# Moving two exact subtractions to TensorE and shortening a hand-built exponential, in an attention and mixture-of-depths kernel

## The chip, the cores and the metric

The kernel runs on one core of a Trainium2 chip. The metric is the device time of one execution in microseconds, the median of several runs. A core has TensorE (PE, matrix products into PSUM), VectorE (DVE) and ScalarE (ACT) for elementwise work, GpSimd (POOL), and SyncE (SP), which here only issues transfers. Each engine takes its own instructions in their order; semaphores hold an instruction until what it reads has been written.

## What is computed

There are B = 8 batches, H = 8 heads, S = 576 positions, 64 elements a head and 32 memory slots. The heads' outputs, side by side, are the rows x of the second part.

```python
a = phi - np.max(phi, axis=2, keepdims=True)
a = np.exp(a)
a = a / (np.sum(a, axis=2, keepdims=True) + 1e-09)
k_m = np.einsum('bhsm,bhsd->bhmd', a, k)
v_m = np.einsum('bhsm,bhsd->bhmd', a, v)
scores = scale * np.matmul(q, k_m.transpose(0, 1, 3, 2))
scores = scores - np.max(scores, axis=-1, keepdims=True)
attn = np.exp(scores)
attn = attn / (np.sum(attn, axis=-1, keepdims=True) + 1e-09)
return np.matmul(attn, v_m).astype(np.float32)
...
scores = np.einsum('bsd,d->bs', x, w_gate)
top_idx = np.argpartition(-scores[b], capacity)[:capacity]
...
ye = np.maximum(xe @ w1, 0.0) @ w2
out[b, top_idx] = x[b, top_idx] + g[:, None] * ye
```

The first softmax runs over the 576 positions, the second over the 32 slots; capacity is 128 of 576 rows. Which 128 rows are chosen depends on the last bits of x. That is why the kernel takes the first softmax and the sums `v_m` with more care than plain float32 products give: it builds its own exponential, and splits both factors of `v_m` into a high part (the low 12 bits masked off) and a low part (the rest).

## The kernel before

**Groups.** The first softmax works on 16 groups, one per batch and half of the heads: a tile of 128 rows (4 heads x 32 slots) and 576 columns. `softmax(i, ch)` (L182 to L279) is a generator; each `yield` ends one of its eleven steps. It takes the maximum and subtracts it (L192, L194), reduces the argument by a multiple q of ln 2 (L197 to L200), and forms exp(r) - 1 as a quotient of two polynomials `num` and `den`. `fma` (L216 to L225) is one step of a polynomial in split arithmetic: six DVE instructions on 128x576, with the high part of the running value in an int16 tile (`vh` or `dh`) that ACT rounds. It is used once for `den` (L229) and three times for `num` (L236). The reciprocal of `den` comes from two squares on ACT, `sq` (L242) and `s2` (L249), with L247 between them, and is applied in L257 and L258. L259 to L276 add the leading part `y0` (an exponential rounded to int16), multiply by the power of two, and divide by the sum. L276 writes the finished group, `e`.

**keys.** `keys` (L308 to L339) goes on from there: PE transposes `e` in six pieces (L316), ACT copies them out of PSUM (L318), DVE masks the high part (L322) and subtracts it to get the low one (L324), GpSimd issues eight stores to `aparts` (L327), and PE forms k_m with float32 products (L333).

**split_v.** `split_v` (L281 to L304) does the same for v, 16 tiles of 128x1152: load, mask (L293), subtract (L295), two stores to `vparts` (L298). Its two tile names have two buffers each.

**values.** `values(st)` (L343 to L383) then sums v_m for two batches at a time, four sets in all: 2304 small products a set (L371), which read both split factors back from memory in 32 pieces (L350, L357).

**The later work.** `attention(b)` makes the second softmax, the outputs and the ranking of the rows, and `ffn` the two weight products (L636, L646) on the chosen rows.

**The order.** Nothing is scheduled by the hardware or a planner: the loop at L747 interleaves the generators turn by turn, and the order of that loop is the order on every engine. In a turn, `softmaxes` takes one step. Two softmax chains run at once for the first eight groups (a new one may start six rounds after the last); the other eight groups run one after another in chain 0. `split_v` takes a step on every odd turn (L755), the value sums take 7, 10 or 12 steps of eight products (L712), and, once chain 1 has ended and all of v is split (L759), `attentions` takes a step, and `ffns` two. The tiles of PSUM named `bank` come from a pool of four buffers, in turn. Because each engine keeps this order, an instruction that waits holds up all that was written behind it, of whatever generator.

Of the kernel before, what the change touches and what calls it, by code (L numbers as in the profile page):

```python
# [8 lines left out]
F32 = mybir.dt.float32  # L9
# [17 lines left out]

LOG2E = 1.44269504088896341
# [5 lines left out]
Y0_SCALE = 12 * 0.6931471805599453  # L34
# [3 lines left out]
def kernel(  # L38
# [76 lines left out]
    make_identity(nc, ident)  # L115

# [52 lines left out]
    UP, GRID = 2.0 ** 23, 2.0 ** -11  # L169
    biases = {}  # L170
    for x in (EXP_P[3] * UP, EXP_P[4] * UP, EXP_P[3] * UP * GRID, EXP_Q[1] * UP,
              EXP_Q[1] * UP * GRID, 127 * UP, -1.5, Y0_SCALE):
        biases[x] = constant(x)
# [8 lines left out]
    def softmax(i, ch):  # L182
# [27 lines left out]
        tt(out=num, in0=num, in1=r, op=ALU.mult)  # L210
        vh = t("vh", I16)
        act(vh, num, GRID, EXP_P[3] * UP * GRID)
        act(num, num, 1.0, EXP_P[3] * UP)
        stt(out=rl, in0=rh, scalar=-GRID, in1=r, op0=ALU.mult, op1=ALU.add)

        def fma(val, h, c):  # L216


            lo, big, low = t("lo"), t("big"), t("low")
            stt(out=lo, in0=val, scalar=GRID, in1=h, op0=ALU.mult, op1=ALU.subtract)  # L220
            tt(out=lo, in0=lo, in1=rh, op=ALU.mult)  # L221
            tt(out=big, in0=h, in1=rh, op=ALU.mult)
            tt(out=low, in0=val, in1=rl, op=ALU.mult)
            tt(out=low, in0=low, in1=lo, op=ALU.add)  # L224
            stt(out=val, in0=big, scalar=c * UP, in1=low, op0=ALU.add, op1=ALU.add)  # L225
# [5 lines left out]
        act(dh, den, GRID / 2)  # L231
        y0 = t("y0", I16)
        act(y0, r, 1.0, Y0_SCALE, AF.Exp)
        for c in (EXP_P[2], EXP_P[1], EXP_P[0]):
            yield
            fma(num, vh, c)  # L236
            if c != EXP_P[0]:
                vh = t("vh", I16)
                act(vh, num, GRID)
            if c == EXP_P[2]:  # L240
                sq = t("rl2")
                act(sq, den, 1.0 / UP, -1.5, AF.Square)  # L242


        dl, p = t("lo"), t("big")
        stt(out=dl, in0=den, scalar=GRID / 2, in1=dh, op0=ALU.mult, op1=ALU.subtract)
        stt(out=p, in0=sq, scalar=0.75, in1=den, op0=ALU.add, op1=ALU.mult)  # L247
        s2 = t("low")
        act(s2, p, 1.0 / UP, -1.5, AF.Square)  # L249
# [7 lines left out]
        stt(out=num, in0=s2, scalar=0.75, in1=num, op0=ALU.add, op1=ALU.mult)  # L257
        stt(out=num, in0=sq, scalar=0.75, in1=num, op0=ALU.add, op1=ALU.mult)  # L258
        stt(out=num, in0=num, scalar=GRID, in1=y0, op0=ALU.mult, op1=ALU.add)  # L259
        sm = ex.tile([P, 4], F32, name="sm")  # L260
        e = t("e")
        stt(out=e, in0=num, scalar=GRID / 2, in1=two_q.bitcast(F32),
# [15 lines left out]
        yield  # L278
        yield from keys(i, ch)  # L279

    def split_v():  # L281
# [6 lines left out]
        coming = load(*groups[0])  # L288
        for i, (b, g) in enumerate(groups):
            vb = coming  # L290
            yield
            hi = vio.tile([P, 4 * S * Dh // P], F32, name="vhi")
            nc.vector.tensor_single_scalar(hi.bitcast(I32), vb.bitcast(I32), -4096,  # L293
                                           op=ALU.bitwise_and)
            nc.vector.tensor_sub(vb, vb, hi)  # L295
            yield
            for vp, src in enumerate((vb, hi)):
                nc.gpsimd.dma_start(  # L298
                    out=vparts[b, g, :, vp].rearrange("w r s d -> w (r s d)")
                                           .rearrange("w (p x) -> p w x", p=P),  # L300
                    in_=src.unsqueeze(1).to_broadcast([P, 2, 4 * S * Dh // P]))
            if i + 1 < len(groups):
                coming = load(*groups[i + 1])
            yield  # L304

    v_m = {}

    def keys(i, ch):  # L308
# [15 lines left out]
        nc.vector.tensor_sub(lo, aS, hi)  # L324
# [422 lines left out]
    while True:  # L747
# [7 lines left out]
        if len(working) == 2 and turn % 2:  # L755
# [71 lines left out]
```

## Time and profile before

| | |
|---|---|
| median of three runs | 1050.5 us (1049.24 to 1057.09) |
| span of the profiled run | 1051.3 us |
| end of L276 for group 1, 5, 9, 16 | 58.3, 216.5, 377.1, 790.5 us |
| v splits (L295) | from 21.3 to 347 us |
| first and last value product | 185 to 937 us, in four sets |
| moved by transfers | 166.11 MB, 158 GB/s over the span |

The end of L276 is the mark to go by: it is the moment at which a group of the first softmax is finished, and everything later (transposes, stores, value sums, attention) waits for it. Up to 377 us two chains share DVE and a group comes about every 40 us; from there to 790 us one chain runs beside attention and the feed-forward part, and a group comes about every 59 us. What follows 790 us has no work of the first softmax in it.

In the lines of the profile, a group names its line, engine, operation, tiles (written <- read) and shape; then come the total and the mean time of one, and the idle time of the engine before it with what ended that. A duration of idle time is a cost only where the engine sets the pace.

### The profile page before, as it was taken

The numbers are of one execution on the slowest core, as the hardware profiler recorded it, in microseconds if no ns is written. First come the engines' busy times: TensorE is split into PE (matmuls) and PEld (weight loads), VectorE is DVE, ScalarE is ACT, GpSimd is POOL, SyncE is SP. The second block draws the span as 40 slices with busy tenths as digits, with TensorE's granted clock in tenths as the row PEclk, the third lists the DMA queues.
The fourth block names the chain that finished last, engine by engine and source line by source line (L and its number), as shares of the span: only waits on it lengthen the run. The fifth ranks groups of instructions, "written<-read, shape, count | busy, mean of one in ns | idle before, by whom it ended". The sixth has DMA issues, their size and how long they took to land. (4 is left out here: it accounts for less than half of the span.)

```text
span 1051.3 us, 25384 instructions
## 1 busy us (share of the span) xinstructions
PE 598.7 (57%) x10738; PEld 439.8 (42%) x10738; DVE 784.4 (75%) x1342; ACT 293.6 (28%) x578; POOL 224.3 (21%) x335
## 2 busy tenths in 40 slices
PE   0021022255554355675567397875738969889795
PEld 0021022154443354554434374664415657544542
DVE  7899999899899968698786968698993336324940
ACT  2233233233233232323224342141432101213230
POOL 7030221220230230404113021402503011011110
PEclk9999999995665656877678699566866986989688
DMA  9364544677887825554613256463404466522320
GB/s 291 126 232 153 188 157 169 192 230 277 264 274 253 313 46 155 152 179 145 214 51 106 72 141 206 127 194 115 114 0 116 153 218 189 163 66 66 120 70 23
DMA packets 60714, 166.11 MB, mean 158 GB/s; under 512 B 10801, under 2 KB 21041, under 8 KB 60593
## 3 DMA queue, kind: packets, MB, share of 16 engines
q1 hardware_dynamic: 39088, 94.14, 29.5%
q0 software_dynamic: 21504, 70.27, 19.7%
q8 instruction: 87, 1.43, 0.6%
q14 instruction: 35, 0.28, 0.1%
HBM read 96.21 MB, written 68.16 MB: 156 GB/s over the span
## 5 line engine op out<-in xcount | busy, mean ns | idle before, releaser
L371 PE MATMUL acc<-a_rows,v_rows 32*64 32x128 f32 x9216 | 217.8, 257 | 106.7 <-DMA a_rows<-aparts 97.6
L371 PEld LDWEIGHTS acc<-a_rows,v_rows 32*64 32x64 f32 x9216 | 197.7, 167 | 150.2 <-issue 113.9
L316 PE MATMUL bank<-ident,e 128*96 128x128 f32 x96 | 22.5, 403 | 214.8 <-DVE e L276 204.6
L316 PEld LDWEIGHTS bank<-ident,e 128*96 128x96 f32 x96 | 16.0, 185 | 219.7 <-issue 183.4
L333 PE MATMUL bank<-lo,kb 96*128 96x64 f32 x384 | 67.0, 353 | 7.6 <-ACT lo L318 6.8
L333 PEld LDWEIGHTS bank<-lo,kb 96*128 96x128 f32 x384 | 65.5, 267 | 12.1 <-ACT lo L318 8.6
L327 POOL DMA_DIRECT2D aparts<-low x64 | 47.2, 746 | 104.5 <-DVE low L324 100.8
L646 PE MATMUL bank<-w_sb,hT 128*128 128x512 f32 x128 | 67.2, 661 | 0.0
L636 PE MATMUL bank<-w_sb,xeT 128*128 128x512 f32 x128 | 65.5, 647 | 2.9 <-ACT xeT L627 2.9
L530 PE MATMUL bank<-vbd,eT 128*128 128x256 f32 x160 | 60.0, 510 | 0.0
L221 DVE TENSOR_TENSOR lo<-lo,rh 128x576 f32<-128x576 f32 x64 | 56.7, 885 | 2.2
L176 ACT ACTIVATE vh<-num 128x576 int16<-128x576 f32 x32 | 21.8, 683 | 127.3 <-DVE num L225 116.7
L534 DVE TENSOR_TENSOR xj<-bank,rd 128x512 f32<-128x512 f32 x40 | 27.5, 688 | 36.8 <-PE bank L530 34.9
L537 POOL TENSOR_TENSOR xj<-xj,mean 128x1024 f32<-128x1024 f32 (+1 forms) x12 | 26.1, 2174 | 128.5 <-DVE xj L534 89.8
L583 DVE SCALAR_TENSOR_TENSOR cmp<-row,tg,wide 128x576 bf16<-128x576 f32 x40 | 32.5, 811 | 25.9 <-ACT row L569 25.1
L298 POOL DMA_DIRECT2D vparts<-vb x16 | 11.6, 726 | 186.2 <-DVE vb L295 161.9
L224 DVE TENSOR_TENSOR low<-low,lo 128x576 f32<-128x576 f32 x64 | 48.5, 758 | 2.2
L327 POOL DMA_DIRECT2D aparts<-big x64 | 46.7, 738 | 0.0
L220 DVE SCALAR_TENSOR_TENSOR lo<-num,vh 128x576 f32<-128x576 f32 x48 | 36.0, 751 | 13.2 <-ACT vh L176 13.2
L530 PEld LDWEIGHTS bank<-vbd,eT 128*128 128x128 f32 x160 | 35.0, 243 | 23.8 <-issue 19.6
L602 PE MATMUL bank<-tg,pick 128*128 128x2 f32 (+1 forms) x80 | 16.9, 329 | 47.4 <-DVE pick L597 20.2
L176 ACT ACTIVATE low<-big,c 128x576 f32<-128x576 f32 x16 | 12.4, 775 | 96.4 <-DVE big L247 96.4
(150 smaller groups left out, 1244.2 us busy)
## 6 DMA issues: line engine op xcount, KB each, us to landing
v_rows<-vparts SPq DMA_DIRECT2D x128, 288.0 KB
vparts<-vb POOLq DMA_DIRECT2D x16, 1152.0 KB, 5.2
vparts<-vhi POOLq DMA_DIRECT2D x16, 1152.0 KB, 8.9
a_rows<-aparts SPq DMA_DIRECT2D x512, 36.0 KB
vb<-in_v SPq DMA_DIRECT2D x16, 576.0 KB
kb<-in_k SPq DMA_DIRECT2D x16, 576.0 KB
qb<-in_qT SPq DMA_DIRECT2D x16, 576.0 KB
out<-xj POOLq DMA_DIRECT2D x16, 512.0 KB, 3.8
```

The lines of the kernel that those rows point to most:

```text
L176: nc.scalar.activation(dst, src, func, bias=biases[c] if c else 0.0, scale=s)
L220: stt(out=lo, in0=val, scalar=GRID, in1=h, op0=ALU.mult, op1=ALU.subtract)
L221: tt(out=lo, in0=lo, in1=rh, op=ALU.mult)
L224: tt(out=low, in0=low, in1=lo, op=ALU.add)
L316: nc.tensor.transpose(out=tp[:, c], in_=a[:, (c0 + c) * PT:(c0 + c + 1) * PT], identity=ident)
L327: nc.gpsimd.dma_start(out=aparts[h, b, g, part].rearrange("(c p) m -> p c m", p=PT), in_=src[:, :, h * M:(h + 1) * M])
L333: nc.tensor.matmul(out=km[:, rr], lhsT=kb[:, c, rr * P:(rr + 1) * P], rhs=aS[:, c, rr * 2 * M:(rr + 1) * 2 * M], start=(c == 0), stop=(c = ...
L371: nc.tensor.matmul(out=accs[i][:Dh, :P].rearrange("p (h m) -> p h m", m=M), lhsT=vr[p, s], rhs=ar[p, :, s], start=(ch == 0 and s == 0), st ...
L530: nc.tensor.matmul(out=o[:, g * 4 * Dh:(g + 1) * 4 * Dh], lhsT=eT[:, g, (c0 + c) * P:(c0 + c + 1) * P], rhs=vbd[b % 3][:, g], start=False, ...
L583: nc.vector.scalar_tensor_tensor(out=cmp, in0=row, scalar=g, in1=wide[:, off:off + S], op0=ALU.is_equal, op1=ALU.mult, accum_out=equal[:, ...
L636: nc.tensor.matmul(out=ps[:n], lhsT=xeT[:, d, :n], rhs=w1_sb[:, d, f0:f0 + 512], start=(d == 0), stop=(d == KD - 1))
L646: nc.tensor.matmul(out=ps[:n], lhsT=hT[:, f, :n], rhs=w2_sb[:, f], start=(f == 0), stop=(f == KF - 1))
```

## The change

There are three parts.

1. **Low parts by TensorE.** A new helper `difference` forms x - y as two accumulated float32 products, x by the identity and y by minus the identity (`less_ident`, made once), 384 columns at a time, and after a `yield` ACT copies the result out of PSUM. It takes the place of the DVE subtraction in `keys` (L324, two pieces of 96x384) and in `split_v` (L295, three pieces of 128x384). The masks stay on DVE. `split_v` now has five steps a tile instead of three, and is called on every turn; `keys` has two steps more.
2. **Softmax.** One of the three split multiply-adds of `num` becomes a plain one (one DVE instruction). The reciprocal of `den` is replaced by two exponentials of r on ACT (`inv`), so L247 and both squares go, and L257 to L259 become a multiplication and an addition. The quotient's grid becomes 2^-14 (`FINE`). In `fma`, the product that does not need the rounded high part moves to the front.
3. **Steps.** The `yield` behind the last softmax instruction goes. With one multiply-add less and two steps more in `keys`, a group still has eleven steps.

```diff
+    less_ident = const.tile([P, P], F32, name="less_ident")
+    nc.scalar.activation(less_ident, ident, AF.Copy, scale=-1.0)
...
         tt(out=num, in0=num, in1=r, op=ALU.mult)
+        stt(out=num, in0=num, scalar=EXP_P[3] * UP, in1=r, op0=ALU.add, op1=ALU.mult)
         vh = t("vh", I16)
-        act(vh, num, GRID, EXP_P[3] * UP * GRID)
-        act(num, num, 1.0, EXP_P[3] * UP)
+        act(vh, num, GRID, EXP_P[2] * UP * GRID)
+        act(num, num, 1.0, EXP_P[2] * UP)
...
             lo, big, low = t("lo"), t("big"), t("low")
+            tt(out=low, in0=val, in1=rl, op=ALU.mult)
             stt(out=lo, in0=val, scalar=GRID, in1=h, op0=ALU.mult, op1=ALU.subtract)
             tt(out=lo, in0=lo, in1=rh, op=ALU.mult)
             tt(out=big, in0=h, in1=rh, op=ALU.mult)
-            tt(out=low, in0=val, in1=rl, op=ALU.mult)
...
-        for c in (EXP_P[2], EXP_P[1], EXP_P[0]):
+        inv = t("rl2")
+        act(inv, r, INV[0], INV[1], AF.Exp)
+        act(inv, inv, 1.0, INV[2] - 9 * LN2, AF.Exp)
+        for c in (EXP_P[1], EXP_P[0]):
...
-            if c == EXP_P[2]:
-                sq = t("rl2")
-                act(sq, den, 1.0 / UP, -1.5, AF.Square)
...
-        stt(out=p, in0=sq, scalar=0.75, in1=den, op0=ALU.add, op1=ALU.mult)
-        s2 = t("low")
-        act(s2, p, 1.0 / UP, -1.5, AF.Square)
...
-        stt(out=num, in0=s2, scalar=0.75, in1=num, op0=ALU.add, op1=ALU.mult)
-        stt(out=num, in0=sq, scalar=0.75, in1=num, op0=ALU.add, op1=ALU.mult)
-        stt(out=num, in0=num, scalar=GRID, in1=y0, op0=ALU.mult, op1=ALU.add)
+        tt(out=num, in0=num, in1=inv, op=ALU.mult)
+        tt(out=num, in0=num, in1=y0, op=ALU.add)
...
         soft[i] = e
-        yield
         yield from keys(i, ch)
...
-            nc.vector.tensor_sub(vb, vb, hi)
-            yield
+            for x0 in range(0, n, n // 3):
+                x = slice(x0, x0 + n // 3)
+                yield from difference(vb[:, x], hi[:, x], vb[:, x])
...
+    def difference(x, y, dst):
+
+        rows, n = x.shape
+        ps = bank([rows, n])
+        nc.tensor.matmul(out=ps, lhsT=ident[:rows, :rows], rhs=x, start=True, stop=False)
+        nc.tensor.matmul(out=ps, lhsT=less_ident[:rows, :rows], rhs=y, start=False, stop=True)
+        yield
+        nc.scalar.activation(dst, ps, AF.Copy)
...
-        nc.vector.tensor_sub(lo, aS, hi)
+        for c0 in range(0, NC, 3):
+            yield from difference(*(x[:, c0:c0 + 3].rearrange("p c m -> p (c m)")
+                                    for x in (aS, hi, lo)))
...
-        if len(working) == 2 and turn % 2:
+        if len(working) == 2:
             next(working[1], None)
```

## The prediction

> **What bounds the kernel now.** I read the page's busy shares first, then the 40 slices, then windows cut at the ends of softmax groups, then the order of VectorE (DVE) inside one group, then the waits.
>
> ```profile
> PE 598.7 (57%) x10738; PEld 439.8 (42%) x10738; DVE 784.4 (75%) x1342; ACT 293.6 (28%) x578; POOL 224.3 (21%) x335
> ...
> PE   0021022255554355675567397875738969889795
> ...
> DVE  7899999899899968698786968698993336324940
> ```
>
> DVE is the busiest engine, but 75% is a mean over unlike phases: nine tenths for the first third, eight tenths until about 790 us, three tenths after that, where TensorE (PE) is at nine tenths. So I cut windows where the softmax of a group writes its last result (L276): groups 1, 5, 9 and 16 of 16.
>
> ```profile
> core 0: us, PE busy (x) PEld busy (x) DVE busy (x) ACT busy (x) POOL busy (x), PEclk, DMA share, GB/s
> 0.00:58.43 58.43, 0.00 (x1) 0.04 (x1) 49.13 (x60) 15.12 (x22) 20.82 (x53) 1.00 0.61 204
> 58.43:216.61 158.18, 32.78 (x289) 29.77 (x289) 146.01 (x223) 47.04 (x77) 33.41 (x46) 1.00 0.56 187
> 216.61:377.22 160.61, 77.80 (x2258) 71.86 (x2259) 147.12 (x234) 46.55 (x82) 35.67 (x53) 0.65 0.75 252
> 377.22:791.80 414.58, 276.35 (x5315) 205.83 (x5316) 337.47 (x595) 131.05 (x269) 99.54 (x123) 0.74 0.44 128
> 791.80:1051.30 259.50, 211.75 (x2879) 132.29 (x2877) 104.67 (x232) 53.86 (x131) 34.90 (x61) 0.84 0.38 119
> ```
>
> Stretches 2 and 3 (groups 2 to 9, about 40 us each) are DVE at 92%. Stretch 4 (seven groups, 59.1 us each) is DVE at 81% with PE at 67%. Stretch 5, a quarter of the time, is PE at 82% and contains no softmax.
>
> ```profile
> 57.46 0.82 DVE L276 SCALAR_TENSOR_TENSOR e<-e,sm,vh 128x576 f32<-128x576 f32 x1
> ...
> 72.65 0.76 DVE L220 SCALAR_TENSOR_TENSOR lo<-num,vh 128x576 f32<-128x576 f32 x1 [0.75 <-ACT vh L176]
> ...
> 77.93 0.76 DVE L220 SCALAR_TENSOR_TENSOR lo<-num,vh 128x576 f32<-128x576 f32 x1 [0.81 <-ACT vh L176]
> ...
> 84.58 0.76 DVE L250 TENSOR_TENSOR big<-y,dh 128x576 f32<-128x576 int16 x1 [0.84 <-ACT low L176]
> ...
> 97.89 0.82 DVE L276 SCALAR_TENSOR_TENSOR e<-e,sm,vh 128x576 f32<-128x576 f32 x1
> ```
>
> This is one group on DVE: 40.4 us from result to result, and only three gaps, 2.4 us together, each for a ScalarE (ACT) result. The waits say who has slack:
>
> ```profile
> PE bank L316 <- DVE e L276: 204.6, 12, 58.4
> ...
> PE acc L371 <- DMA a_rows<-aparts: 97.6, 47, 13.3
> ...
> ACT lo L318 <- PE bank L316: 25.6, 13, 5.6
> ```
>
> PE waits for the softmax 204.6 us in all. In stretch 3 that slack is only 2 to 12 us a group, beside some 9 us a group of waits for transfers.
>
> **What the Trainium skill says.** "VectorE: DVE Perf Modes", the perf-mode tier table: an fp32 tensor_tensor has only the one-element mode, an fp32 tensor_scalar the double one. The trace agrees: for the same 1152 elements the subtraction L295 takes 1358 ns, the masking L293 765. So the dear half of each split moves. "TensorE: Matmul & The Clock Gate", Part 1: the array runs at half clock until about 3.4 us of sustained activity. The trace agrees in size: 24 records of L333 took 5.38 us at 60.99 and 2.79 us at 614.25; but 5.4 us of work there did not warm it. The same page, Architectural detail: ACT and DVE are strict FIFO, PE pulls only weight loads ahead. Every wait above fits that, though no row proves it. "ScalarE: Activation LUTs", What ACT_TABLE_LOAD costs: only a switch of table set costs, 1283 ns; the trace has one load, of 1283 ns, for exponential, tanh and sign alike, so two more exponentials add none.
>
> **The change part by part, per group.** *Softmax on DVE.* One of four multiply-adds (L220 to L225) goes: 0.751+0.885+0.750+0.750+0.758+0.758 = 4.65 us. L247 goes: 0.75. L257 to L259 (0.749+0.885+0.758 = 2.39) become two tensor_tensors at 0.758: 0.88 less. One plain multiply-add of 0.76 is added. Net 5.5 us. *Waits.* L247's square was what L250 waited for (0.84); of the three later vh waits (two of them exposed, 0.75 and 0.81), one goes with its multiply-add, and in the rest a product that doesn't need vh (0.75) is moved into the gap. Together 2.4 us. *Splits.* L324 (0.954) and L295 (1.358) leave DVE: 2.3 us. So 7.8 us of DVE work and 2.4 us of gaps per group; 16 x 7.8 = 125 us of 784, all on the engine that sets the pace of stretches 1 to 4.
>
> *ACT.* Two squares become two exponentials of the same cost (760 and 775 ns rows). One vh (0.68) goes. Five evictions of 384 columns come (L318's row: 0.484): 2.42. Net 1.7 us a group, 28 in all, on an engine at 28%: hidden, as time.
>
> *PE.* No 384-column fp32 product is in the trace. L636 is 128 records of 512 columns for 64 products, so two passes each, and 16 records took 7.13 us at full clock: 0.446 a pass, 0.334 for 384 columns. A difference is two products, four passes: 1.34 us warm, and with L333's ratio of 1.93, 2.6 us cold. Three per v split, two per group: 6.7 to 13 us a group. I take a middle, near 9, in stretches 2 and 3 and the warm price later. In stretch 2 PE is busy 8.2 us a group (32.78 / 4); with 2.4 v splits and the keys, all cold, that is 8.2 + 2.4 x 7.8 + 5.2 = 32 us, just beside DVE's; warm it is half. In stretch 3 it doesn't fit freely.
>
> *The new waits.* Each eviction makes ACT wait for PE, and behind it in ACT's queue stand the next group's rh, num, den and vh, for which DVE waits. And with the yield after L276 removed, the masking of keys (L322) has only the two L200s (1.5 us) to cover transposes and both evictions; those took from 58.28 to about 61.0, 2.7 us. So about 1.2 us of DVE stall a group there. For ACT's blocking nothing in the trace gives a size: from 0 to 8 us a group (two differences and L333 cold, one behind another); I take 3 in stretch 2, 5 in stretch 3, where the value sums stand in PE's queue too.
>
> *The schedule.* v is split on every turn, five turns a group instead of six, so 2.4 a softmax group instead of 2. The load of v then leads its masking by two turns of some 2.8 us, where it led by four of 3.3; DVE's wait for it is between 0 and 5 us a split (the two stored parts land in 5.2 and 8.9 us now). I take 0, since DMA at 0.56 in stretch 2 has room, and leave the rest to the range. A difference also holds one of four PSUM banks over a turn; I cost that at nothing, since the matching eviction is the very wait counted above. The softmax keeps its eleven steps, so the sums, attention and feed-forward per group stay: by the instruction order 6912 value products are done before the last softmax in both kernels. Stretch 5 keeps its content; I give it 261 us (260.8 now, plus one eviction).
>
> *The sum.* Group 1: 58.3 - 5.5 - 2.4 - 2.7 (two v splits) + 1 = 48.7. Stretch 2: DVE's floor is 39.5 - 5.5 - 1.0 - 2.7 (two v splits a group) - 2.4 + 0.3 (more masking) = 28.3, say 29; plus 1.2 and 3: 33.5 each, four make 134. Stretch 3: DVE 29 + 1.2 + 5 = 35; PE 19.5 busy + 9 of DMA waits + 4 for keys + 4 for the last v splits = 36.5. The larger: 36.5, four make 146. Stretch 4: 59.1 - 6.5 - 2.4 + 1.2 + 1.9 (half of the new PE work, in turns where PE is full) = 53.3, seven make 373. Sum 48.7 + 134 + 146 + 373 + 261 = 963 us.
>
> **The rivals.** *All of the DVE time arrives* (no stall, PE and ACT keep up): 47.7 + 8 x 29 + 7 x (59.1 - 8.9) + 261 = 892. For it: PE waits 204.6 us for the softmax. Against: that slack lies mostly before 180 us. *The coupling eats half*: stretches at 37, 41 and 57 us a group: 49 + 148 + 164 + 399 + 261 = 1021. For it: PE in stretch 3 is nearly as long as DVE already, at clock 0.65; in stretch 4 attention already holds DVE for PE. *PE takes over as the bound and it is slower*: cold products, late sums and ACT blocked behind them give 40, 48 and 61: 50 + 160 + 192 + 427 + 263 = 1092. For it: 16 x 13 us is 208 us of cold PE work. Against: ACT waited only 25.6 us for the transposes, which stand in the same queue, and denser work should warm the clock.
>
> **How the numbers follow.** 963 has 0.60, 892 has 0.10, 1021 has 0.22, 1092 has 0.08. The predicted time is 963. Low 905 lies near the no-stall case (group stalls of 4 to 5 us gone in stretches 2 and 3, and 3 in stretch 4); high 1030 takes in the half-eaten one. Outside is some 0.18. Faster by over 1% is under 1040: 0.88; within 1%: 0.05; slower: 0.07.
>
> **What would show it.** Right: DVE busy near 660, ACT near 322; groups 2 to 5 at 31 to 36 us; L316's wait for e reduced to a few us in stretch 3; a last part of about 260 us after group 16. Wrong: DVE waiting for ACT num, vh or q by over 5 us a group (blocked ACT), DVE waiting at the masking of v for a load, group times in stretch 4 unchanged (PE is its bound), or a last part that grows because work was only put off.

## The result, and the profile after

The changed kernel takes 1012.7 us (median; 1007.5 to 1017.4), beside 1049.9 us for the kernel before on the same chip: a ratio of 0.9637, with a 95% interval from 0.9566 to 0.9707. The forecast was 963. The direction was right and the time lies in the range, but the gain is 37 us where 87 were forecast. The question is where the other 50 went. Medians are of fast runs only, so one slower run of "k_m copied late" is left out of its median.

First the page after, the busy shares and the slices of PE and DVE:

```profile
PE 711.1 (70%) x11058; PEld 478.1 (47%) x11058; DVE 664.5 (65%) x1198; ACT 318.6 (31%) x643; POOL 222.5 (22%) x336
...
PE   3357655856666476767785797769669777889795
...
DVE  7999998456486766784979667794952435225940
```

DVE lost 119.9 us of work (784.4 to 664.5), about what was forecast, yet the span fell by 36 us only. The time in which DVE is not busy grew from 266.9 to 351.1 us. The row of DVE says where: its nines used to last for a third of the span, and now they end after a sixth and give way to digits from 4 to 8. No engine is near its limit in its place: PE's row shows mostly 5s to 7s there.

Then the windows after, cut as before at the last softmax result (now L277) of groups 1, 5, 9 and 16; the columns are named in the first line:

```profile
core 0: us, PE busy (x) PEld busy (x) DVE busy (x) ACT busy (x) POOL busy (x), PEclk, DMA share, GB/s
0.00:46.10 46.10, 11.41 (x20) 5.49 (x21) 39.68 (x49) 13.93 (x22) 20.00 (x52) 0.82 0.71 237
46.10:169.20 123.10, 72.98 (x257) 43.04 (x256) 113.99 (x186) 58.04 (x106) 36.89 (x50) 0.76 0.77 261
169.20:350.80 181.60, 116.29 (x2524) 85.97 (x2524) 113.11 (x188) 56.04 (x105) 32.24 (x46) 0.74 0.67 214
350.80:747.10 396.30, 289.26 (x5354) 204.47 (x5354) 291.84 (x541) 134.84 (x274) 96.51 (x126) 0.78 0.46 134
747.10:1015.60 268.50, 221.19 (x2904) 139.11 (x2904) 105.88 (x237) 55.75 (x136) 36.84 (x62) 0.84 0.38 116
```

Stretch 2 is what was hoped for: 30.8 us a group, DVE at 93%. Stretch 3 got longer than it was before (181.6 us for 160.6), though its DVE work fell from 147 to 113 us: DVE is at 62% and PE at 64%. Stretch 4 is 56.6 us a group for 59.1. The last part, with no softmax in it, grew by 8 us (268.5 for 260.8; the prediction's window for it begins at 791.80, 1.3 us behind the end of group 16 at 790.5).

The table has the stretches of all kernels of this study, in us a group for the middle three (4, 4 and 7 groups), with the span of the profiled execution. The windows of each are cut at its own results, and each row is one execution.

| kernel | group 1 | stretch 2 | stretch 3 | stretch 4 | last part | span |
|---|---|---|---|---|---|---|
| before | 58.3 | 39.5 | 40.2 | 59.1 | 260.8 | 1051.3 |
| forecast | 48.7 | 33.5 | 36.5 | 53.3 | 261 | 963 |
| after | 46.1 | 30.8 | 45.4 | 56.6 | 268.5 | 1015.6 |
| softmax alone | 47.5 | 32.1 | 37.0 | 54.5 | 260.8 | 966.3 |
| softmax, keys on PE | 44.1 | 32.9 | 38.7 | 56.9 | 259.4 | 987.9 |
| softmax, v on PE | 47.6 | 31.1 | 41.8 | 54.0 | 260.0 | 977.7 |
| rows kept | 46.0 | 30.8 | 34.8 | 56.2 | 269.7 | 971.1 |
| k_m copied late | 46.0 | 30.3 | 43.8 | 56.4 | 266.0 | 1003.6 |
| v loads by GpSimd | 55.0 | 51.1 | 48.5 | 56.6 | 263.0 | 1112.3 |
| products on constants | 48.0 | 33.3 | 39.9 | 56.4 | 268.8 | 1004.4 |
| keys' steps only | 44.1 | 33.5 | 40.9 | 55.4 | 263.2 | 992.8 |
| keys' constants | 44.1 | 33.5 | 41.3 | 57.0 | 262.2 | 1004.2 |
| v on PE, first 11 tiles | 47.5 | 31.0 | 36.4 | 54.5 | 263.5 | 961.6 |
| softmax, k_m late | 50.6 | 32.1 | 36.9 | 55.0 | 259.1 | 970.8 |
| the same in ten steps | 47.2 | 33.4 | 40.0 | 50.2 | 280.3 | 972.7 |
| v two ahead | 46.0 | 30.5 | 42.3 | 56.6 | 267.0 | 1000.2 |
| v two ahead, k_m late | 46.0 | 30.4 | 41.3 | 56.6 | 266.7 | 995.4 |
| softmax, v two ahead | 47.5 | 32.1 | 36.6 | 54.9 | 259.4 | 966.0 |
| 11 tiles, v two ahead | 47.5 | 31.1 | 35.2 | 55.8 | 266.2 | 969.5 |

What DVE waits for in stretch 3 (line and tile, what released it; us in total, times, the longest), before:

```profile
DVE lo L220 <- ACT vh L176: 5.4, 7, 0.8
DVE big L250 <- ACT low L176: 3.4, 4, 0.8
```

and after:

```profile
DVE lo L227 <- ACT vh L181: 30.1, 4, 13.1
DVE vhi L293 <- DMA vb<-in_v: 21.6, 5, 9.5
DVE big L332 <- ACT lo L328: 10.1, 4, 4.5
DVE num L215 <- ACT num L181: 2.8, 3, 1.1
```

Two small waits for ACT became three large ones: for the rounded high part `vh` (7.5 us a group), for the load of v, and for the transposed keys. The waits of PE and ACT in the same stretch of the kernel after:

```profile
PE acc L383 <- DMA a_rows<-aparts: 33.5, 9, 9.0
ACT kbd L350 <- PE bank L345: 31.5, 4, 13.2
...
PE bank L311 <- DMA vb<-in_v: 18.8, 4, 7.0
...
PE bank L326 <- DVE e L277: 0.9, 1, 0.9
```

PE's own work (116.3 us) and its two waits for transfers (33.5 for rows, 18.8 for v) come to 168.6 of the 181.6 us. For DVE it waits only 0.9 us here. ACT's wait for k_m was 4.5 us in this stretch before:

```profile
ACT kbd L338 <- PE bank L333: 4.5, 3, 1.7
```

The wait of ACT at L350 (31.5 us) and that of DVE for `vh` (30.1 us) are nearly the same wait, as one case in the timeline shows (start, duration, instruction, and in brackets the idle time before it; PE's, then ACT's, then DVE's):

```profile
187.23 0.48 PE L383 MATMUL acc<-a_rows,v_rows 32*64 32x128 f32 x8 [4.63 <-DMA a_rows<-aparts]
187.64 1.65 PE L311 MATMUL bank<-vb,ident 128*128 128x384 f32 x2
189.08 1.49 PE L312 MATMUL bank<-vhi,less_ident 128*128 128x384 f32 x2
190.50 1.76 PE L383 MATMUL acc<-a_rows,v_rows 32*64 32x128 f32 x56
192.19 5.38 PE L345 MATMUL bank<-lo,kb 96*128 96x64 f32 x24
...
197.60 0.45 ACT L350 ACTIVATE kbd<-bank 64x64 f32<-64x64 f32 x2 [13.20 <-PE bank L345]
198.08 0.49 ACT L314 ACTIVATE vb<-bank 128x384 f32<-128x384 f32 x1
198.46 0.68 ACT L181 ACTIVATE vh<-num 128x576 int16<-128x576 f32 x1
...
199.17 0.76 DVE L227 SCALAR_TENSOR_TENSOR lo<-num,vh 128x576 f32<-128x576 f32 x1 [13.13 <-ACT vh L181]
```

PE waits 4.63 us for rows of the value sums. Behind them in its queue stand a difference of v, more sums, and k_m (L345), which takes 5.38 us. ACT has the copy of k_m at the head of its queue from 184.4 us on, and behind it `vh`, which needs nothing from PE. DVE needs `vh`. So DVE stands for 13.13 us behind a late transfer of 4.63 us and PE's own work in front of the copy, half of which is L345 (5.38 us here, 2.79 us at 738.11 us in a kernel shown further below). The strict order of ACT's queue, for which the prediction cited the Trainium skill, "TensorE: Matmul & The Clock Gate", Architectural detail, is here to be seen: `vh` starts when the copies ahead of it, with which it has nothing to do, are done.

SyncE's queue is tied to PE as well. Its largest wait in this stretch, after and then before:

```profile
SPq L362 <- PE acc L383: 33.2, 12, 9.8
...
SPq L350 <- PE acc L371: 27.1, 9, 10.8
```

A reload of rows waits until PE has used up a buffer, and the load of the next v stands behind it in the one queue. So PE waits for transfers that wait for PE. That tie was there before; new are PE's products that need the load of v, and the faster pace at which v is split.

PE's waits over the whole span, beside those shown of before: the wait for the softmax (L326, was L316) fell from 204.6 to 65.9 us, and a wait for the mask of v is new (none of it lies in stretch 3).

```profile
PE acc L383 <- DMA a_rows<-aparts: 81.5, 36, 9.0
PE bank L326 <- DVE e L277: 65.9, 10, 15.0
PE bank L312 <- DVE vhi L293: 37.4, 6, 17.7
```

### The profile page after: what moved, and what is told of

It reads as the page before. It is cut to its first block, busy times and chain, and to the rows that moved or that the text cites. A ratio compares the mean times of both kernels' runs of the same rounds, so it can differ in the third digit from the quotient of the medians.

```text
span 1015.6 us, 26006 instructions
## 1 busy us (share of the span) xinstructions
PE 711.1 (70%) x11058; PEld 478.1 (47%) x11058; DVE 664.5 (65%) x1198; ACT 318.6 (31%) x643; POOL 222.5 (22%) x336
## 5 line engine op out<-in xcount | busy, mean ns | idle before, releaser
L383 PE MATMUL acc<-a_rows,v_rows 32*64 32x128 f32 x9216 | 205.3, 247 | 86.4 <-DMA a_rows<-aparts 81.5
L383 PEld LDWEIGHTS acc<-a_rows,v_rows 32*64 32x64 f32 x9216 | 184.5, 156 | 143.3 <-issue 73.0
L312 PE MATMUL bank<-vhi,less_ident 128*128 128x384 f32 x96 | 51.9, 631 | 43.9 <-DVE vhi L293 37.4
L311 PE MATMUL bank<-vb,ident 128*128 128x384 f32 x96 | 52.8, 640 | 34.1 <-DMA vb<-in_v 21.2
L326 PE MATMUL bank<-ident,e 128*96 128x128 f32 x96 | 20.5, 374 | 76.8 <-DVE e L277 65.9
L658 PE MATMUL bank<-w_sb,hT 128*128 128x512 f32 x128 | 66.8, 658 | 0.0
L326 PEld LDWEIGHTS bank<-ident,e 128*96 128x96 f32 x96 | 14.8, 174 | 84.9 <-issue 84.1
L312 PEld LDWEIGHTS bank<-vhi,less_ident 128*128 128x128 f32 x96 | 22.8, 246 | 65.6 <-DVE vhi L293 43.4
L345 PEld LDWEIGHTS bank<-lo,kb 96*128 96x128 f32 x384 | 52.0, 218 | 3.4 <-issue 2.0
L345 PE MATMUL bank<-lo,kb 96*128 96x64 f32 x384 | 52.7, 302 | 0.0
L339 POOL DMA_DIRECT2D aparts<-big x64 | 46.7, 738 | 11.8 <-DMA vparts<-vhi 5.7
L227 DVE SCALAR_TENSOR_TENSOR lo<-num,vh 128x576 f32<-128x576 f32 x32 | 28.4, 888 | 31.5 <-ACT vh L181 31.5
L311 PEld LDWEIGHTS bank<-vb,ident 128*128 128x128 f32 x96 | 21.3, 246 | 47.4 <-issue 29.3
L542 PEld LDWEIGHTS bank<-vbd,eT 128*128 128x128 f32 x160 | 35.2, 244 | 17.1 <-issue 12.9
L273 ACT ACTIVATE vh<-e,sm 128x576 f16<-128x576 f32 x16 | 12.4, 776 | 91.6 <-DVE sm L268 91.6
```

What stands on the lines that cost most here:

```text
L311: nc.tensor.matmul(out=ps, lhsT=ident[:rows, :rows], rhs=x, start=True, stop=False)
L312: nc.tensor.matmul(out=ps, lhsT=less_ident[:rows, :rows], rhs=y, start=False, stop=True)
L326: nc.tensor.transpose(out=tp[:, c], in_=a[:, (c0 + c) * PT:(c0 + c + 1) * PT], identity=ident)
L339: nc.gpsimd.dma_start(out=aparts[h, b, g, part].rearrange("(c p) m -> p c m", p=PT), in_=src[:, :, h * M:(h + 1) * M])
L345: nc.tensor.matmul(out=km[:, rr], lhsT=kb[:, c, rr * P:(rr + 1) * P], rhs=aS[:, c, rr * 2 * M:(rr + 1) * 2 * M], start=(c == 0), stop=(c = ...
L383: nc.tensor.matmul(out=accs[i][:Dh, :P].rearrange("p (h m) -> p h m", m=M), lhsT=vr[p, s], rhs=ar[p, :, s], start=(ch == 0 and s == 0), st ...
```

## The experiments

Two theories went in. **The ring:** in stretch 3 PE, ACT, DVE and SyncE wait for one another in turn (rows, difference, copy, `vh`, mask), so that waits add up that I had laid side by side. **PE's work:** the extra products are simply too much for PE at a granted clock of 0.74. Diffs are against the changed kernel.

### The parts alone

**The softmax alone.** Both subtractions go back to DVE; the second and third `yield` keep a group at eleven steps.

```diff
-            for x0 in range(0, n, n // 3):
-                x = slice(x0, x0 + n // 3)
-                yield from difference(vb[:, x], hi[:, x], vb[:, x])
+            nc.vector.tensor_sub(vb, vb, hi)
+            yield
...
-        for c0 in range(0, NC, 3):
-            yield from difference(*(x[:, c0:c0 + 3].rearrange("p c m -> p (c m)")
-                                    for x in (aS, hi, lo)))
+        nc.vector.tensor_sub(lo, aS, hi)
...
-        if len(working) == 2:
+        if len(working) == 2 and turn % 2:
...
         soft[i] = e
+        yield
...
+        yield
         for c in (EXP_P[1], EXP_P[0]):
```

> Only the softmax part of the change; both subtractions stay on DVE, v split on odd turns, eleven steps a group kept by two empty yields. Ring theory (in stretch 3, groups 6 to 9, the value sums' reloads hold PE, PE's order holds ACT at the copy of k_m, ACT holds DVE's vh): groups 2 to 5 at 32 to 33 us, but groups 6 to 9 still at 41 to 45 us, total 1000 to 1015 us. PE-work theory (the new fp32 products overfill PE in stretch 3): without them groups 6 to 9 come down to 32 to 35 us, total 960 to 980 us.

Measured: 971.9 us, a ratio of 0.9217 (0.9167 to 0.9267) to the kernel before. The windows of its stretches 3 and 4:

```profile
175.80:323.80 148.00, 76.49 (x2282) 70.47 (x2282) 126.84 (x207) 44.09 (x78) 36.28 (x53) 0.65 0.83 280
323.80:705.50 381.70, 275.65 (x5310) 202.55 (x5310) 298.52 (x544) 127.61 (x260) 98.48 (x122) 0.75 0.47 139
```

The softmax part gives 80 us, and the other two parts, low parts on PE and steps, then cost 41. That is the main finding. It also went against the ring as I had first stated it: by that, any kernel with faster softmax would be caught in stretch 3 by the reloads, at 41 to 45 us a group and 1000 to 1015 us in all. It is at 37.0, with DVE at 86% although DVE has 13.7 us more work there than after. PE waits even longer for rows there than after (60.6 us at L382 for 33.5), but DVE has enough work to set the pace. So the reloads alone don't make stretch 3 long; something of the other two parts, products or order of steps, belongs to it.

**Keys on PE, v on DVE**, and **v on PE, keys on DVE.** The first undoes only the edits of `split_v` and its turn:

```diff
-            for x0 in range(0, n, n // 3):
-                x = slice(x0, x0 + n // 3)
-                yield from difference(vb[:, x], hi[:, x], vb[:, x])
+            nc.vector.tensor_sub(vb, vb, hi)
+            yield
...
-        if len(working) == 2:
+        if len(working) == 2 and turn % 2:
```

> The change with the subtraction of v put back on DVE and v split on odd turns as before; keys stay on PE. Ring theory: DVE pays 1.36 us a split again, groups 2 to 5 at 33 us; groups 6 to 9 at 40 to 44 us, because value sums and k_m copy are as they were; total within 1% of the change (1003 to 1022 us). PE-work theory: three quarters of the new PE work before the end of group 9 is gone, so groups 6 to 9 at 34 to 37 us, total 975 to 990 us. Theory of the v loads (held up behind the row loads, since v is split in shorter steps): waits at the masking of v vanish, stretch 3 shorter by some 20 us.

The second undoes only those of `keys` and the steps:

```diff
-        for c0 in range(0, NC, 3):
-            yield from difference(*(x[:, c0:c0 + 3].rearrange("p c m -> p (c m)")
-                                    for x in (aS, hi, lo)))
+        nc.vector.tensor_sub(lo, aS, hi)
```

> The change with the subtraction of keys put back on DVE (eleven steps a group kept by two empty yields); v stays on PE. From the run with softmax alone and the run with v on DVE: keys on PE cost 2.4 us a group in stretch 4 and little in stretch 2. If the two parts cost what they cost apart: stretch 2 at 30 us, stretch 3 at 42 to 44 us, stretch 4 at 54.5 us a group; total 985 to 997 us. If v's cost in stretch 3 needs the keys' products as well: stretch 3 at 37 to 39 us, total 970 to 980 us.

Measured: 990.7 us (0.9402, 0.9377 to 0.9427) with the keys on PE, 979.6 us (one timing) with v on PE. From the softmax alone, the keys cost 18.8 us and v another 22.0. By the table the keys cost it in stretch 4 (7 x 2.4 = 17 us), stretch 3 (7) and stretch 2 (3), less 3 in group 1. v, added to that, costs 27 us in stretch 3 (4 x 6.7) and 9 in the last part, and gives 8 in stretch 2. v alone raises stretch 3 by 4.8 a group, both together by 8.4. Neither run decides between the theories: the first lies between both forecasts, and the second has the whole time of its second forecast with a stretch 3 near its first. Both edits also move steps; which part of the cost is the products' and which the order's is asked further below.

### Stretch 3

**Rows kept.** The first set of the value sums loads only three of its 32 pieces of rows and goes on with what stands in the buffers; every product is still made.

```diff
-            if ch + 2 < n:
+            if ch + 2 < n and (st or ch == 0):
                 load(ch + 2)
```

> The change, with the value sums of set 0 (batches 0 and 1) leaving out the reload of 29 of their 32 pieces: the products run on pieces 0 to 2 again and again, so v_m of two batches is another number. All other work is there. Ring theory: PE waits no more for rows and SyncE's queue is free, so DVE's idle time in stretch 3 falls from 65 us to under 20 and groups 6 to 9 to 31 to 35 us; total 965 to 980 us. PE-work theory: the products and differences are all still there, groups 6 to 9 stay at 41 us or more, total 1000 to 1015 us.

Measured: 972.9 us (one timing); stretch 3 fell from 45.4 to 34.8 us a group, and nothing else moved. DVE's waits in its stretch 3:

```profile
DVE lo L227 <- ACT vh L181: 10.4, 4, 4.2
DVE big L332 <- ACT lo L328: 7.4, 4, 3.3
DVE num L215 <- ACT num L181: 3.2, 4, 1.1
DVE vhi L293 <- DMA vb<-in_v: 1.4, 1, 1.4
```

With every product still on PE, the waits for `vh` and the load of v fell from 51.7 to 11.8 us. The number of PE's products is not what makes stretch 3 long: 34.8 us a group is less than the forecast. PE also had a granted clock of 0.83 for 0.74 and was busy 100.4 us for 116.3 with the same 2524 products, so some of the gain is the clock's. The reloads are one necessary part; the softmax alone, at 37.0, shows that they need something of the other two parts beside them.

**The products on constants.** DVE subtracts v as before, and PE and ACT make the same three differences a tile out of a weight, into a tile that nobody reads.

```diff
+            nc.vector.tensor_sub(vb, vb, hi)
+            scratch = vio.tile([P, n // 3], F32, name="scratch", bufs=1)
-            for x0 in range(0, n, n // 3):
-                x = slice(x0, x0 + n // 3)
-                yield from difference(vb[:, x], hi[:, x], vb[:, x])
+            for _ in range(3):
+                yield from difference(wg[:, :n // 3], wg[:, D - n // 3:], scratch)
```

> The change with v subtracted on DVE again, and beside it the same PE products and ACT copies as the change has for v, in the same places, but on a constant tile, into a scratch tile that nobody reads. So PE has the work, but waits neither for a load of v nor for its mask. If the PE time of the differences is what stretch 3 loses: groups 6 to 9 at 44 to 48 us (1.4 us a split more on DVE). If it is PE's new waits for v: groups 6 to 9 at 38 to 41 us, as with v on DVE (38.7).

Measured: 1006.2 us (one timing); stretch 3 at 39.9. That is 1.2 us above the kernel with v on DVE, so the time of the products and copies, and the step on every turn, cost little here. The other 5.5 us of v's 6.7 a group come from what differs: with v itself in the products, PE waits for its load (18.8 us in stretch 3, none here) and holds up everything behind, and the stores of v wait for ACT's copies. These two are not separated. The whole time is hardly better than after because DVE has its 1.36 us a tile back and stretch 2 is 2.5 us a group longer.

**k_m copied late.** The two copies of k_m (L350) are written three turns later, so that ACT no longer stands at them.

```diff
-        for u in range(2):
-            part = slice(u * Dh, (u + 1) * Dh)
-            nc.scalar.activation(kbd[b][part, 2 * g:2 * g + 2, u * M:(u + 1) * M],
-                                 km[part, :, u * M:(u + 1) * M], AF.Copy)
+        late.append((turn + 3, b, g, km))
...
+        while late and late[0][0] <= turn:
+            copy_kbd(*late.pop(0)[1:])
         for _ in range(steps()):
```

> The change, with the copy of k_m out of PSUM on ACT written three turns later, so that it doesn't stand in front of the rounding vh that DVE waits for. Ring theory: DVE's wait for vh in stretch 3 falls from 30 us to under 8, and stretch 3 from 181 us to 155 to 170; total 988 to 1005 us. Pure row-loop theory (the reloads alone set the pace of stretch 3): the wait moves to another place and stretch 3 stays within 5 us of 181; total within 1% of the change.

Measured: 1001.4 us (0.9503, 0.9462 to 0.9543). The wait for `vh` fell from 30.1 to 6.0 us, and the waits for the load of v (21.6 to 31.1) and at L332 (10.1 to 13.6) grew: 6 of 182 us are gained. One tie opened, the wait moves to the next.

**v loads by GpSimd.** The load of v leaves the queue in which the row loads stand.

```diff
-            nc.sync.dma_start(out=vb, in_=v[b, g])
+            nc.gpsimd.dma_start(out=vb, in_=v[b, g])
```

> The change, with the loads of v issued from GpSimd's queue, so that they don't stand behind the loads of rows in SyncE's. If it is the queue of the v loads that costs stretch 3 its time: DVE's waits at the masking of v fall from 21.6 us to under 5 and groups 6 to 9 come to 39 to 41 us; total 993 to 1000 us. If it is the PE time of the v differences between the value products: the waits move to vh, groups 6 to 9 stay at 43 us or more; total within 1% of the change.

Measured: 1114.1 us (one timing), worse than the kernel before. DVE's wait for v in stretch 2, where it had been 0.5 us, became 68.2; a load took 9.3 us from issue to landing (the median), and it now stood behind the stores of the previous parts, which wait for ACT. That made v late everywhere and says nothing on the row loads. The next one asks the question better.

**v two ahead**, and **the same with k_m late.** A third buffer for v, and its loads issued two tiles ahead.

```diff
-            vb = vio.tile([P, 4 * S * Dh // P], F32, name="vb")
+            vb = vio.tile([P, 4 * S * Dh // P], F32, name="vb", bufs=3)
...
-        coming, n = load(*groups[0]), 4 * S * Dh // P
+        coming, n = [load(*g) for g in groups[:2]], 4 * S * Dh // P
...
-            vb = coming
+            vb = coming.pop(0)
...
-            if i + 1 < len(groups):
-                coming = load(*groups[i + 1])
+            if i + 2 < len(groups):
+                coming.append(load(*groups[i + 2]))
```

> The change, with a third buffer for v and each load written one whole split earlier, so that it stands ahead of more row loads in SyncE's order. If it is the place of the v loads behind the row loads that makes DVE and PE wait for v: DVE's wait at the masking of v in stretch 3 falls from 21.6 us to under 5, and groups 6 to 9 come to 39 to 42 us; total 990 to 1003 us. If the loads are late for the memory's sake (transfers busy): the wait stays above 15 us and the total within 1% of the change.

The other has this and the edit of "k_m copied late".

> As the run before, and the copy of k_m on ACT three turns later as well. With the late copy alone the wait for vh went (30 to 6 us) and the wait for v grew (22 to 31 us). If these two places are where the ring of waits closes: with both opened DVE is idle under 30 us in stretch 3, groups 6 to 9 at 35 to 38 us, total 980 to 992 us. If the pace of stretch 3 is the value sums' reloads alone: the wait moves once more and groups 6 to 9 stay at 42 us or more.

Measured: 1002.0 and 997.2 us (one timing each). Two ahead takes the wait for the load to nothing, and the wait for `vh` grows from 30.1 to 38.6 us: 42.3 us a group. With both edits DVE waits in stretch 3 for

```profile
DVE big L332 <- ACT lo L328: 21.7, 4, 8.9
DVE lo L227 <- ACT vh L181: 17.8, 3, 7.0
DVE e L263 <- ACT den L181: 6.1, 1, 6.1
```

so that 41.3 us are left, 4.3 above the softmax alone and between the two forecasts. All of these are for ACT. I did not find which tie holds this rest; it may be several. PE waits for rows 41.4 us in it.

### Stretch 4

**Keys' steps only**, and **keys' products on constants.** Both have v on DVE. In the first, DVE subtracts for the keys, but the order of the changed kernel, with its two late steps in `keys` and none behind the softmax, stays. The second makes the keys' products and copies on constants besides.

```diff
-        for c0 in range(0, NC, 3):
-            yield from difference(*(x[:, c0:c0 + 3].rearrange("p c m -> p (c m)")
-                                    for x in (aS, hi, lo)))
+        nc.vector.tensor_sub(lo, aS, hi)
+        yield
+        yield
```

> The run with v on DVE, with the subtraction of keys on DVE too, but the change's steps in keys: no yield behind e, two yields after the mask. No product of the change is left on PE; against the run with softmax alone only the place of two steps differs. If keys cost stretch 4 its 2.4 us a group by the order of steps alone: stretch 4 at 56 to 57 us a group. If by the products and their copies: 54 to 55 us, total 965 to 977 us.

```diff
+        nc.vector.tensor_sub(lo, aS, hi)
+        for _ in range(2):
+            yield from difference(wg[:PT, :384], wg[:PT, D - 384:], const_scratch)
```

> As the run before, and in the two steps the change's products and copies of keys, but on a constant tile into a scratch tile: PE and ACT have the work, PE waits for no mask, and the stores wait for DVE's subtraction alone. If PE's and ACT's time costs stretch 4: 56.5 to 58 us a group (0.95 us a group more on DVE than with keys on PE). If PE's wait for the mask and the later stores cost it: 54 to 55.5 us.

Measured: 994.7 and 1006.1 us (one timing each). In stretch 4 the softmax alone has 54.5 us a group; the order of steps takes it to 55.4, the products on constants to 57.0, while the keys on PE have 56.9 with 0.95 us less on DVE. Kernels that have the softmax's steps and the keys on DVE differ there among themselves, from 54.0 (v on PE) to 55.8 (11 tiles, v two ahead). So the 0.9 us of the order are not clear of that scatter; the 1.6 us from the time of PE and ACT are the likelier part of the keys' 2.4, and why the 0.95 us saved on DVE don't show is not explained. The cost is to be seen in DVE's waits of stretch 4. The softmax alone has

```profile
DVE xj L545 <- PE bank L541: 19.5, 6, 6.8
DVE ph L205 <- ACT q L181: 8.6, 4, 4.2
...
DVE rd L533 <- PE bank L528: 6.7, 2, 4.8
```

and with the keys on PE

```profile
DVE xj L545 <- PE bank L541: 35.1, 11, 7.8
DVE ph L205 <- ACT q L181: 17.0, 4, 8.0
DVE rd L533 <- PE bank L528: 13.6, 4, 9.8
```

DVE waits here for attention's products (L541, L528) and for ACT's `q`; over the three rows from 34.8 to 65.7 us. Taking work off DVE and giving it to PE is no gain where DVE waits for PE. The order of steps alone costs 3.9 us a group in stretch 3 too (40.9 for 37.0), with 25.1 us of waits for the load of v, and in all it takes 994.7 us, where the keys' products on PE have 990.7 and the softmax alone 971.9. So the 18.8 us put down to the keys above are not shown to be the cost of their products: the order of two steps alone costs about as much. The ten steps below, also without a subtraction on PE, have 40.0 in stretch 3 and 21.6 us of waits for that load. What is shown to cost time in stretch 3 by its place on PE is the subtraction of v (45.4 us a group, for 39.9 with the products on constants).

### A better kernel

**v on PE for the first 11 tiles**: where PE is idle v goes to it, later to DVE, and the keys stay on DVE.

```diff
+            if i < 11:
                 for x0 in range(0, n, n // 3):
                     x = slice(x0, x0 + n // 3)
                     yield from difference(vb[:, x], hi[:, x], vb[:, x])
+            else:
+                slow.append(i)
+                nc.vector.tensor_sub(vb, vb, hi)
+                yield
...
-        for c0 in range(0, NC, 3):
-            yield from difference(*(x[:, c0:c0 + 3].rearrange("p c m -> p (c m)")
-                                    for x in (aS, hi, lo)))
+        nc.vector.tensor_sub(lo, aS, hi)
...
-        if len(working) == 2:
+        if len(working) == 2 and (turn % 2 or not slow):
```

> The softmax part, keys on DVE, and v subtracted on PE only for the first 11 of 16 tiles, those that come before the value sums start; the other five on DVE, on odd turns. If the differences are a gain where PE is idle and a loss where the value sums run: group 1 at 46 us, groups 2 to 5 at 30 to 31 us, groups 6 to 9 at 35 to 37 us, stretch 4 at 54.5 us a group, last part 261 us: 950 to 962 us, below the 972 us of the softmax part alone. If v on PE costs as much anywhere: 970 us or more.

Measured: 969.0 us (0.9229, 0.9185 to 0.9272). Stretch 2 gains the 1.1 us a group that PE can take for nothing, 4 us in all, which can't be told from the softmax alone by the times. The stretches came as expected, but the profiled execution was the fastest of six, and the median misses the expected 950 to 962 us.

**The softmax alone with k_m late** (the two edits of above together), and **the same in ten steps** (without the `yield` ahead of the loop over `EXP_P`).

```diff
-        yield
         for c in (EXP_P[1], EXP_P[0]):
             yield
```

> The softmax part alone, with the copy of k_m on ACT three turns later. If ACT held at that copy costs time there as well: stretch 3 from 37.0 to 35 or 36 us a group, and the wait for q in stretch 4 (8.6 us) gone, total 955 to 967 us. If these waits only move: 968 to 975 us, as without it.

> As the run before, without the empty yield ahead of the loop over the two multiply-adds, so a group has ten steps and stretch 4 takes ten turns a group. If DVE sets stretch 4: its groups shorten by a turn's share of attention (some 2 us each), and the last part grows by as much work put off: total 955 to 970 us. If work put off into the last part costs more there, where PE is full: above 975 us.

Measured: 975.1 us (0.9267, 0.9194 to 0.934) and 973.4 us (0.9249, 0.9189 to 0.9309). The late copy brings nothing where ACT isn't held up. Ten steps shorten stretch 4 to 50.2 us a group, and the last part grows to 280.3: with fewer turns a group less of the later work is done beside the softmax, and it comes back behind it.

**The softmax alone, v two ahead**, and **the 11 tiles, v two ahead**: the edits of above together, of which the first line is

```diff
-            vb = vio.tile([P, 4 * S * Dh // P], F32, name="vb")
+            vb = vio.tile([P, 4 * S * Dh // P], F32, name="vb", bufs=3)
```

> The softmax part alone with the v loads one split earlier. There the wait for v is 4.1 us in all in stretch 3: at most 1 us a group to gain, 967 to 973 us; if earlier loads only crowd the transfers, the same or up to 5 us more.

> The softmax part, the first 11 tiles of v on PE, and v loads one split earlier. Without the earlier loads: 31.0, 36.4 and 54.5 us a group, 969 us. If the wait for v (3.4 us in stretch 3) is all that the loads cost: 963 to 970 us.

Measured: 968.4 us (0.9225, 0.9164 to 0.9286) and 968.6 us (0.9195, 0.9152 to 0.9238). These two, the softmax alone and the 11 tiles can't be told apart; all are some 4% below the changed kernel. I would keep the simplest, the softmax alone.

## Why the prediction was right, and where it was wrong

**Right: what each part costs by itself.** DVE's work was forecast at 660 us and is 664.5; ACT's at 322, and is 318.6. A difference of 384 columns was priced at 1.34 us warm and 2.6 cold: from start to start of the instruction behind, it took 1.37 us in one kernel (736.30 to 737.67) and 2.81 in another (750.89 to 753.70). PE's waits for rows in stretch 3 were taken at 9 us a group and are 8.4 (33.5 / 4); that is partly luck, for the wait is no fixed price: it is 15.2 with the softmax alone (60.6 / 4). Three small slips: 29 + 1.2 + 3 is 33.2, not 33.5; the evictions behind group 1 end at 61.3 us, not 61.0; and the first value product of the kernel before starts at 197.6 us, after a wait from 184 us on (the table ahead of the prediction has 185).

**Right: stretch 2, a little better than thought.** Its DVE work is 28.5 us a group (113.99 / 4), for 28.3 and "say 29". The stalls were taken at 1.2 + 3 us and are 2.3 ((123.10 - 113.99) / 4); at L332 there are 0.4 us in all. PE was busy 18.2 us a group, near the warm end (16) of what the prediction allowed. With group 1 this is 13 us less than forecast.

**Wrong: stretch 3, +35.6 us, the largest part of the miss.** The step that failed is "Stretch 3: DVE 29 + 1.2 + 5 = 35; PE 19.5 busy + 9 of DMA waits + 4 for keys + 4 for the last v splits = 36.5. The larger: 36.5". The work was about right: DVE's is 28.3 us (113.11 / 4), and PE's 29.1 (116.29 / 4) for 27.5. The waits were not. The load of v was put at nothing ("I take 0", with a bound of 5 us): it cost DVE 5.4 us a group (21.6 / 4), and PE, whose products need the same load and for which the sum has no such term, 4.7 (18.8 / 4). ACT's blocking, taken at 5, is 8.2 ((30.1 + 2.8) / 4, `vh` and `num`), and the wait at the mask of keys, taken at 1.2, is 2.5 (10.1 / 4). With the measured terms PE's sum is 42.2 us and DVE's 44.4, of 45.4. The argument "DMA at 0.56 in stretch 2 has room" looked at the transfers' load, but the load of v stands in SyncE's queue behind row loads that wait for PE (33.2 us).

Nor are the two sums independent, as "the larger" has it. ACT's copies wait for PE, that of k_m above all, and DVE's `vh` stands behind them, so PE's waits for transfers come back as waits of DVE. Taking the wait for the load away (v two ahead) gained only 3.1 us a group (45.4 to 42.3), since the wait for `vh` grew by 2.1 ((38.6 - 30.1) / 4). That PE waits for DVE in return, which would close a ring, is not shown: in stretch 3 it did so for 0.9 us. What the waits show closed is the loop of PE and the reloads, which was there before (27.1 us of SyncE's waits for PE), and into which v's load and products now fall. That the reloads are needed for the loss is shown by leaving them out (34.8 us a group); that v's products add to it is shown by the products on constants (39.9) and by v on DVE (38.7). The order of the keys' steps costs some of the rest (40.9 for 37.0, with no subtraction on PE); how the last 4 us divide among the single ties is not settled.

**Wrong: stretch 4, +23 us.** Here the failing term is the 2.4 us of gaps that would close in each group. The forecast for the softmax's share was 59.1 - 5.5 - 2.4 = 51.2; the softmax alone has 54.5. DVE's work fell by the 5.5 (48.2 to 42.6 us a group), but the time in which it isn't busy rose, from 11.0 to 11.9 ((414.58 - 337.47) / 7 and (381.70 - 298.52) / 7). The gaps for ACT were read in a group of stretch 2, and there they close (12.2 us before, 3.7 with the softmax alone, over four groups). In stretch 4 they were smaller from the start: the waits for `vh` (1.6 us) and at L250 (5.9) are 1.1 us a group over seven groups, and DVE waits for attention instead, the longer with a shorter softmax (for L541's products 19.5 us, 15.5 before; at `eT` 6.1, 0.5 before). The price for the keys there, -0.95 + 1.2 + 1.9 = +2.15, was right as a sum (+2.1 from the softmax alone to the changed kernel), but not in its terms: the 1.2 us more at the mask of keys did not come (3.9 us over seven groups, 4.5 before), and what came in its place is not fully explained (see the keys' constants).

**Wrong: the last part, +7.5 us.** It was to stay, and grew by 9 us over the kernel with v on DVE, which has the same instructions there. Some 5 of the 9 us are lost in the first 33 us (from the start of this part's PE work to the first record of L658, 747.15 to 779.97 us, for 728.60 to 756.21 at L657 with v on DVE), and there the clock that PE was granted was lower. The windows behind the last softmax result, after,

```profile
747.10:772.00 24.90, 24.85 (x77) 15.09 (x78) 7.27 (x23) 6.26 (x17) 7.93 (x10) 0.61 0.39 102
```

and with v on DVE:

```profile
728.50:753.50 25.00, 23.64 (x170) 14.18 (x170) 8.20 (x28) 8.70 (x22) 9.05 (x15) 0.85 0.42 111
```

PE is busy nearly all the time in both, at 0.61 of the full clock after and at 0.85 with v on DVE. Why the clock differs, and where the other 4 us went, was not found.

**The rival "the coupling eats half"** gave 1021 us, the nearer number, and named PE's load in stretch 3 and attention's hold on DVE in stretch 4, at 0.22. It put the loss in stretch 3 at 41 us and gave nothing back in stretch 2; a stretch 3 that was 18 us longer (182 for 164) and a last part 7.5 us longer stand against a stretch 2 that was 25 us shorter (123 for 148) in its sum.

## What to carry to other kernels

Before work is moved to an engine that looks idle, write down whom it will wait for and what stands behind it in both queues; then add to each engine's work every wait it will have before you take the larger, above all one for a transfer that is issued from a queue which waits for the same engine. Two engines at 62% and 64%, none near its limit, are a reason to write up such a sum for each. And forecast and try the parts of a change one at a time, the order of steps among them: here one part was worth 80 us, and the other two cost half of it.

## What was not expected of the hardware

The clock of PE after a pause. In both kernels compared above, PE had waited about 9 us and then worked nearly without a pause. With v on DVE, the same pair of products (L310) took 1.59 us at first and 0.89 us from 8 us after the start on:

```profile
728.60 1.49 PE L325 MATMUL bank<-ident,e 128*96 128x128 f32 x6 [8.71 <-DVE less L600]
...
732.33 1.59 PE L310 MATMUL bank<-lo,ident 96*96 96x384 f32 x2
...
736.30 0.89 PE L310 MATMUL bank<-lo,ident 96*96 96x384 f32 x2
...
738.11 2.79 PE L344 MATMUL bank<-lo,kb 96*128 96x64 f32 x24
```

After, the same work in the same order was still at half the speed 16 us after the start: L345 takes 5.22 us for 2.79, and the four products of L484 behind it 1.23 us, while the same four took 0.71 us with v on DVE (at 740.83).

```profile
747.15 1.49 PE L326 MATMUL bank<-ident,e 128*96 128x128 f32 x6 [9.79 <-DVE less L601]
...
754.86 1.59 PE L311 MATMUL bank<-lo,ident 96*96 96x384 f32 x2
...
758.38 5.22 PE L345 MATMUL bank<-lo,kb 96*128 96x64 f32 x24
763.53 1.23 PE L484 MATMUL bank<-qb,kbd 128*64 128x288 f32 x4
```

The Trainium skill, "TensorE: Matmul & The Clock Gate", Part 1, gives about 3.4 us of sustained work for the full clock. The measurement decides: it took 8 us once (728.60 to 736.30), and more than 16 another time (747.15 to 763.53). What else kept the clock down was not tested.

The queue that issues a load mattered: the same 576 KB of v, issued by GpSimd behind its stores, cost 68.2 us of DVE waits in stretch 2 where they had cost 0.5 in SyncE's queue.
